# Two loads and a batch's scores moved by some steps in a fused attention and gated feed-forward kernel

## The chip, the cores and the metric

One core of a Trainium2 chip runs the whole program. The metric is device time in microseconds of one execution; lower is better. The core has a matrix engine (TensorE, PE in the profile), VectorE (DVE), ScalarE (ACT), GpSimd (POOL) and SyncE (SP), which in this kernel issues all DMA transfers of the main loop, in program order, from one queue.

## The reference

Eight batches, 12 heads, 448 positions, head size 64, all float32. Scores of all heads are mixed by a 12 x 12 matrix before the softmax, the weights of all heads by another behind it; the result goes through a feed-forward part with a gate and two matrices behind it.

```python
scores = scale * np.matmul(q, k.transpose(0, 1, 3, 2))
scores = np.einsum('bhij,hg->bgij', scores, w_pre)
scores = scores - np.max(scores, axis=-1, keepdims=True)
attn = np.exp(scores)
attn = attn / (np.sum(attn, axis=-1, keepdims=True) + 1e-09)
attn = np.einsum('bhij,hg->bgij', attn, w_post)
x = np.matmul(attn, v)          # then heads side by side: 3584 x 768
a = x @ w1
b = x @ w2
out = (a * b @ w3) @ w_out
```

The feed-forward weights come from the host as 64-bit words, which the kernel itself turns into float32 and splits into two parts.

## The kernel before

**Steps.** The attention part runs in steps `n`, 45 for each batch (`NB`), in one loop at the end of `run`. A step stands for a tile of ten query rows of one batch, all 12 heads. Work goes through HBM once: the scores of two heads at a time are computed and stored to `raw_d`, and the tiles are read back with the heads on the partitions, so that one matmul mixes them.

**Score units.** `qk` (L165 to L187) computes one unit (b, p, c): batch b, head pair p, query block c of 128 rows (c = 3 takes the last 64 rows of two pairs). Eight matmul instructions (L173) fill two PSUM banks, two ScalarE copies (L178, L179) take them to an SBUF tile `st`, and a store to `raw_d` follows (L187; for c = 3 two stores, L184). The store is put on the list `later` and issued at the start of the next step. The second unit of a step uses banks 6 and 7, the first banks 0 and 1. The tile `st` has two buffers in the pool `kp`; units of the first batch with an odd p have two others, in `qp`. A batch has 21 units; six of the first one (c = 0) come before the loop.

**Their places.** `qks` lists the units of each step, `loads` the loads of their inputs (`kq`, L156), six steps ahead of the unit with c = 0. The first batch's other 15 units lie on steps 0 to 14. The second batch's begin at `first` and lie `per` steps apart: steps 11, 12, 13, 15, 16, 17, 19, 20, 21 and so on to 37. Later batches have 45 / 21 steps for a unit.

**Tiles.** Each even step begins with a fetch (L201) of two tiles from `raw_d`, four steps ahead of their use. `mix` (L219), `largest` (L226, VectorE), `exp` (L234, ScalarE), `scale` (L243 to L246), `post` (L259) and `put` (L273) then work on a pair of tiles over two to three steps.

**Values.** `load_v` (L285) loads the values of one head pair of the next batch on a list. Steps 6 to 11 each load one for the first batch; later ones are loaded when their predecessor was used for the last time. `av` (L300) uses them in steps 19 and 21 first.

**Weights.** Beside the attention, w3 and w_out are folded into one matrix (`psf`, L359) in the steps up to 48. Their words come in 40 loads (`cs`, L100), at most one a step, two steps ahead of the conversion, into three buffers. The conversion of one load is a ScalarE square (L106), four VectorE instructions (L116 to L120), a ScalarE cast and a GpSimd subtraction (L125, L126). A step with `av` takes none. From step 18 on the fold's matmuls are shared out by `shares`: each step gets a number that levels the TensorE work, with a weight of 3.7 for a score unit, 5.1 for an `av` and 9.3 for the odd steps' `post`; before, they follow the conversions (`there`). Step 50 (`SWITCH`) ends the fold; from step 53 the experts (`eg`) take its place.

**Order in one step**, as far as it matters here: fetch (even steps); everything on `later` (stores of the step before); the other inputs of the first batch or `load_v`; `load_kq`; the load of weight words; conversion; fold matmuls and `exp`; `av`; `post` and `mix` (odd steps); the step's score units. The kernel gives the order of all engines by hand: nothing is reordered behind it.

Of the kernel before, what the change touches and what calls it, by code (L numbers as in the profile page):

```python
# [17 lines left out]
HP = H // 2  # L18
IB = 10
GI = H * IB  # L20
NB = -(-S // IB)
# [28 lines left out]
class Kernel:  # L50
# [689 lines left out]
    def run(self):  # L740
# [64 lines left out]
        for n, u in enumerate([(0, p, c) for c in (1, 2) for p in range(HP)] + [(0, p, 3) for p in range(1, HP, 2)]):  # L805
            qks[n] = [u]
        for b in range(1, B):
            first, per = (11, 28 / 21) if b == 1 else ((b - 1) * NB - 6, NB / 21)
            units = [(b, p, c) for g in range(0, HP, 2) for p, c in [*itertools.product((g, g + 1), range(3)), (g + 1, 3)]]
            for i, (b, p, c) in enumerate(units):  # L810
                n = int(first + i * per) | (b > 1)
                qks.setdefault(n, []).append((b, p, c))
                if c == 0:
                    loads.setdefault(max(n - 6, 0), []).append((b, p))
        for b in range(B):
            for a in range(NG):
                for g in range(HP):
                    n = (b * NB + (a + 1) * GB + 3) | 1
# [25 lines left out]
        for pair in range(ONE // 2, B // 2 - 1):  # L844
            first = P_AT if pair == ONE // 2 else 2 * NB * (pair + 1) + 13
# [5 lines left out]
        def advance(count):  # L851
            nonlocal done
            for _ in range(min(count, total - done)):
                next(background)
                done += 1
                self.age += len(self.ends) > 0
                if self.age > 2:
                    self.do_ends()

        def there(p):  # L860

            f, r = divmod(p - 3 - 2 * KF, 3)
            return 2 * KF * 3 * (1 + f) + (0, 9, 18)[r] if f >= 0 else min(max(3 * (p - 3), 0), KF * 3)
# [3 lines left out]
        def others(p):  # L867
            nc.sync.dma_start(self.kqs[0, p][:, QT + S:], self.kq0[p][:, QT + S:])
# [19 lines left out]
        for n in range(N + 6):  # L888
            self.step, third = n, False
            if n == GB + 1:  # L890
                self.close("qp")
                self.xp = [self.pool("xp0", 1)]
            if n == SWITCH:
                assert done == total
                next(background, None)
                self.do_ends()
                self.do_soon()
                self.do_later()
                assert not fold_pieces
                self.close("fp")  # L900
                self.wp = self.pool("wp", 5, side="right")
                self.up = self.pool("up", 1, side="right")
                self.xp.append(self.pool("xp1", 1, side="right"))
                background, total, done = self.experts(phases), (E_1 + E_2) * ONE + P_1 * (B - ONE) // 2, 0
            if n == LATE:
                assert done >= E_1
                self.close("xp0", "cx")
                self.xq, self.cb = self.pool("xq", 2), self.pool("cb", 1)
            if n == PAIR:

                assert done >= 2 * E_1 + E_2 and unit_pieces is None and not self.jobs and not self.ys
                self.do_ends()
                self.do_soon()
                self.do_later()
                self.pairs, self.w_ahead = True, 4
                self.close("xp1", "cb", "xq", "cs")
                self.xq = self.pool("xq", 2)
                self.up2 = self.pool("up2", 1, side="right")
                self.free += range(N_UP, NS)
                setup = self.pair_setup(phases)  # L920
            if PAIR <= n < PAIR + 7:
                next(setup, None)
            m, odd = divmod(n, 2)
            if not odd and LF <= n + LF < N:
                self.fetch(m + LF // 2)
            self.do_later()
            if n + 3 < HP:
                others(n + 3)
            elif HP <= n < 2 * HP:
                self.load_v()  # L930
            for x in loads.get(n, []):
                self.load_kq(*x)

            p, pieces = self.n_made - 1 if fold_pieces else 2 * KF + 3 * KF, None
            if avs.get(n):
                pass
            elif fold_pieces:
                f = (self.n_made - 1 - 2 * KF) // 3
                if f < 2 or done >= 2 * KF * 3 * (f - 1):
                    pieces = fold_pieces  # L940
                    if next(pieces, self) is self:
                        fold_pieces = pieces = None
            if m < SETS:
                if odd:
                    self.scale(m)
                else:
                    self.largest(m)
            self.do_soon()
            if pieces:
                next(pieces)  # L950
            elif unit_pieces and not fold_pieces and not avs.get(n):
                ahead = 1 if n < SWITCH else 2 * done // (3 * K1) + 4 + (done > 0)
                if n_pieces < ahead:
                    n_pieces += 1
                    if next(unit_pieces, self) is self:
                        unit_pieces = None
                    else:
                        next(unit_pieces)
                        third = True
            now = share.get(n, 0)  # L960
            if n < SWITCH:

                wanted += now
                now = max(min(there(p), KF * 3 + wanted) - done, 0)
            self.do_sums()

            advance(now // 2)
            self.do_ends()
            if not odd and m < SETS:
                self.exp(m)  # L970
            advance(now - now // 2)
            for x in avs.get(n, []):
                self.av(*x)
            self.do_ends()
            if odd and 1 <= m <= SETS:
                self.post(m - 1)
            if odd and m + 1 < SETS:
                self.mix(m + 1)
            self.do_ends()
            for i, x in enumerate(qks.get(n, [])):  # L980
                self.later.append(self.qk(*x, (6, 7) if i else (0, 1)))
            if third:
                next(unit_pieces)
# [67 lines left out]
```

## Time and profile before

| | |
|---|---|
| runs | 1459.4, 1459.1, 1453.31 us |
| median | 1459.1 us |
| the profiled execution | 1456.61 us, its span 1454.8 us |
| TensorE busy, 0 to 146 us | 113.73 us |
| TensorE busy, 146 to 437 us | 279.99 of 291 us |
| TensorE busy, 437 to 1200 us | 746.80 of 763 us |
| TensorE busy, 1200 to 1455 us | 249.61 of 255 us |
| mean granted clock of TensorE | 0.985 of full speed |

A profile is of one execution. The page gives the busy time of each engine and, in 40 slices, where in the span it lies; windows give the same for chosen stretches with the granted clock and what DMA moved. Waits are put down to what came last. "DMA share" is the mean busy share of the 16 DMA engines, and can be somewhat above 1. Matmul records are in part missing from a trace.

### The profile page before, as it was taken

The page shows a single profiled execution, that of the slowest core. Times are in us where ns is not written, and L with a number is a line of the kernel's source. Part 1 is how long each engine was busy: PE and PEld are TensorE (multiplying, and loading weights), DVE is VectorE, ACT ScalarE, POOL GpSimd, SP SyncE. Part 2 cuts the span into 40 slices and gives each one's busy share as a digit, 9 for nine tenths or more (in the row PEclk, how much of TensorE's full clock was granted, in tenths as well). Part 3 has the DMA queues.
Part 4 walks back from the last instruction along what each step waited for, and adds up shares of the span by engine and source line. Part 5 has one row for each costly group of instructions (what it writes and reads, how often), then busy time and mean ns, then how long its engine had stood idle before and what let it go on. Part 6 is the DMA issues. An engine that isn't in the chain of part 4 may idle for free.

```text
span 1454.8 us, 45722 instructions
## 1 busy us (share of the span) xinstructions
PE 1390.1 (96%) x18684; PEld 1059.4 (73%) x18684; DVE 739.0 (51%) x1497; ACT 833.1 (57%) x1952; POOL 620.7 (43%) x754
## 2 busy tenths in 40 slices
PE   5789998999999989999999999999999999999998
PEld 2357785776677667776777777777776777899988
DVE  4867565767644544432344445334444447334563
ACT  3876665777756656665555656656655546422231
POOL 1333232444324434632244445444335446446683
PEclk7989998999999999999999999999999999999999
DMA  8998789999999999999989988799879766698875
GB/s 256 365 319 274 237 267 287 311 336 307 316 288 353 348 343 319 368 338 314 311 266 291 319 278 280 234 312 350 288 230 285 236 179 214 206 332 263 240 229 173
DMA packets 203760, 416.86 MB, mean 287 GB/s; under 512 B 20528, under 2 KB 120112, under 8 KB 203472
## 3 DMA queue, kind: packets, MB, share of 16 engines
q1 hardware_dynamic: 203552, 413.94, 87.2%
q8 instruction: 149, 2.44, 0.7%
q14 instruction: 59, 0.48, 0.1%
HBM read 279.77 MB, written 134.09 MB: 284 GB/s over the span
## 4 chain that ended last, share of the span: by engine, by line
PE 78%; DMA 13%; DVE 5%; ACT 3%; issue 1%; SPq 0%; POOL 0%; DVEq 0%; ACTq 0%; POOLq 0%
PE e L701 20%; PE psa L300 10%; PE pso L259 10%; PE psm L219 8%; PE psq L173 7%; PE psf L359 5%; PE eg L521 4%; PE e2o L701 4%; PE e1o L701 4%; PE e3o L701 4%; DMA s_d<-s 3%; PE eo L552 3%; DMA cs<-wo 3%; DMA r<-raw_d 2%; DMA wu<-w_d 2%; ACT e L234 1%
## 5 line engine op out<-in xcount | busy, mean ns | idle before, releaser
L246 POOL TENSOR_SCALAR w<-wpo,ri 128x60 f32<-128x60 f32 x360 | 180.7, 518 | 489.0 <-DVE ri L244 465.8
L226 DVE TENSOR_REDUCE mn<-psm 128x1 f32<-128x448 f32 x360 | 207.8, 619 | 317.0 <-PE psm L219 316.6
L701 PE MATMUL e<-eh,wu 128*128 128x448 f32 x1008 | 297.3, 372 | 6.3 <-DVE c L655 3.2
L273 ACT COPY mt<-pso 128x480 f32<-128x480 f32 x352 | 197.8, 621 | 177.3 <-PE pso L259 177.1
L234 ACT ACTIVATE e<-psm,mn 128x448 f32<-128x448 f32 x360 | 226.6, 642 | 9.6 <-DVE mn L226 9.6
L219 PE MATMUL psm<-r,wsc 60*64 60x448 f32 (+1 forms) x1440 | 197.9, 557 | 32.1 <-ACT e L234 19.9
L701 PEld LDWEIGHTS e<-eh,wu 128*128 128x128 f32 x1008 | 188.0, 188 | 52.5 <-issue 27.4
L259 PEld LDWEIGHTS pso<-w,e 60*64 60x64 f32 x10080 | 174.5, 134 | 50.0 <-issue 44.0
L259 PE MATMUL pso<-w,e 60*64 60x60 f32 x10080 | 198.6, 224 | 0.1
L701 PE MATMUL e<-el,wu 128*128 128x448 f32 x504 | 187.1, 371 | 0.0
L173 PE MATMUL psq<-kq 64*64 64x448 f32 x1176 | 159.5, 546 | 0.6 <-ACT st L178 0.6
L300 PE MATMUL psa<-mt,v 128*64 128x150 f32 (+1 forms) x2304 | 156.9, 293 | 1.9 <-ACT st L178 1.9
L300 PEld LDWEIGHTS psa<-mt,v 128*64 128x64 f32 x2304 | 143.6, 137 | 17.9 <-issue 6.3
L655 DVE TENSOR_TENSOR c<-c,e 128x448 f32<-128x448 f32 x168 | 101.8, 618 | 87.6 <-PE e L701 82.8
L178 ACT COPY st<-psq 128x448 f32<-128x448 f32 x162 | 86.4, 533 | 68.8 <-ACT mt L273 32.8
L521 PE MATMUL eg<-xh,wu 128*128 128x448 f32 x384 | 118.8, 380 | 4.8 <-DMA wu<-w_d 4.8
L640 POOL TENSOR_TENSOR el<-x,eh 128x448 fp32r<-128x448 f32 x90 | 104.2, 1176 | 34.8 <-ACT eh L639 34.8
L701 PEld LDWEIGHTS e<-el,wu 128*128 128x128 f32 x504 | 94.9, 188 | 22.4 <-issue 14.1
L243 DVE TENSOR_SCALAR sa<-sm 128x2 f32<-128x2 f32 x180 | 35.9, 200 | 129.6 <-ACT e L234 129.0
L173 PEld LDWEIGHTS psq<-kq 64*64 64x64 f32 x1176 | 62.2, 136 | 53.8 <-issue 29.8
L521 PEld LDWEIGHTS eg<-xh,wu 128*128 128x128 f32 x384 | 71.8, 190 | 38.1 <-issue 25.3
L179 ACT COPY st<-psq 128x448 f32<-128x448 f32 x162 | 87.7, 541 | 0.0
(99 smaller groups left out, 2011.5 us busy)
## 6 DMA issues: line engine op xcount, KB each, us to landing
r<-raw_d SPq DMA_DIRECT2D x344, 210.0 KB, 4.9
raw_d<-st SPq DMA_DIRECT2D x138, 448.0 KB, 5.4
wu<-w_d SPq DMA_DIRECT2D x104, 384.0 KB, 6.4
wu<-s_d SPq DMA_DIRECT2D x96, 384.0 KB, 4.8
wu<-w_d SPq DMA_DIRECT2D x51, 512.0 KB, 5.6
kq<-kq SPq DMA_DIRECT2D x42, 448.0 KB, 6.2
wu<-s_d SPq DMA_DIRECT2D x36, 512.0 KB, 4.9
x<-x_d SPq DMA_DIRECT2D x72, 224.0 KB, 6.3
```

The source lines that it names most:

```text
L173: nc.tensor.matmul(ps[s][z * PP:(z + 1) * PP], t[rows, q:q + PP], t[rows, k:k + S], start=True, stop=True)
L219: nc.tensor.matmul(ps[s][c * PP:(c + 1) * PP, :S], self.wsc[k], r[k, c], start=True, stop=True)
L226: self.nc.vector.tensor_reduce(mn[:, s:s + 1], self.psm[m][s][:, :S], axis=AX.X, op=ALU.min)
L234: nc.scalar.activation(e, p[:, :S], AF.Exp, bias=mn[:, s:s + 1], scale=-1.0, accum_out=sm[:, s:s + 1])
L246: nc.gpsimd.tensor_scalar_mul(w2[:, s], self.wpo, ri[:, s:s + 1])
L259: nc.tensor.matmul(self.pso[c][z * PP:(z + 1) * PP, at:at + HK], e[k, j * PP:(j + 1) * PP], w2s[k, s], start=True, stop=True)
L273: self.nc.scalar.copy(dst.rearrange("p j g (s i) -> p j s g i", s=2), src)
L300: nc.tensor.matmul(self.psa[rows, g % 3, :W], v[:, j, rows], mt[:, j, 2 * g + s, :W], start=(j == 0), stop=(j == NJ - 1))
L521: nc.tensor.matmul(p, u[:, k % (K1 // 2), x], xs[y][:, k], start=(k == 0 and t == 0), stop=(k == K1 - 1 and t == 2))
L640: nc.gpsimd.tensor_tensor(lo, x, hi.bitcast(F32), op=ALU.subtract)
L655: nc.vector.tensor_tensor(a[out], a[to[0]], p, op=ALU.add)
L701: nc.tensor.matmul(p, w[:, k, x], ops[m, k][y], start=(k == 0 and t == 0), stop=(k == nk - 1 and t == 2))
```

## The change

The second batch's units begin at step 14 in place of 11 and lie 1.2 steps apart in place of 28 / 21 = 1.33. Their loads of `kq` move along. `load_v` is called in steps 11 to 16 in place of 6 to 11.

```diff
@@ -805,7 +805,7 @@
         for n, u in enumerate([(0, p, c) for c in (1, 2) for p in range(HP)] + [(0, p, 3) for p in range(1, HP, 2)]):
             qks[n] = [u]
         for b in range(1, B):
-            first, per = (11, 28 / 21) if b == 1 else ((b - 1) * NB - 6, NB / 21)
+            first, per = (14, 1.2) if b == 1 else ((b - 1) * NB - 6, NB / 21)
             units = [(b, p, c) for g in range(0, HP, 2) for p, c in [*itertools.product((g, g + 1), range(3)), (g + 1, 3)]]
             for i, (b, p, c) in enumerate(units):
                 n = int(first + i * per) | (b > 1)
@@ -926,7 +926,7 @@
             self.do_later()
             if n + 3 < HP:
                 others(n + 3)
-            elif HP <= n < 2 * HP:
+            elif HP <= n - 5 < 2 * HP:
                 self.load_v()
             for x in loads.get(n, []):
                 self.load_kq(*x)
```

## The prediction

> **What bounds the kernel now.** I read the page first, for the stage; then the DMA queue's timeline, for the places of the steps in time; then windows of two steps each; then the waits and the chain inside them.
>
> ```profile
> span 1454.8 us, 45722 instructions
> PE 1390.1 (96%) x18684; PEld 1059.4 (73%) x18684; DVE 739.0 (51%) x1497; ACT 833.1 (57%) x1952; POOL 620.7 (43%) x754
> PEclk7989998999999999999999999999999999999999
> DMA  8998789999999999999989988799879766698875
> ```
>
> TensorE is busy 96% of the span, so only its idle time and slow clock can be won: 64.7 us in all, and the change reaches only the beginning. Slices of 36.4 us: the steps that it touches, 5 to 38, lie in slices 2 to 6.
>
> ```profile
> 40.09 1.28 SPq L201 DMA_DIRECT2D r<-raw_d  x2
> ...
> 66.22 0.38 SPq L367 DMA_DIRECT2D w_d<-fz  x1
> ...
> 71.29 1.40 SPq L201 DMA_DIRECT2D r<-raw_d  x2
> 72.99 1.32 SPq L187 DMA_DIRECT2D raw_d<-st  x2
> ...
> 94.81 1.24 SPq L201 DMA_DIRECT2D r<-raw_d  x2
> ```
>
> Each even step begins with a fetch (L201). The two stores at 72.99 are those of step 11, the first step with two score units, and stores go out one step later; so 71.29 is step 12, 40.09 is step 4 and 94.81 step 18. Windows from fetch to fetch, with columns PE, PEld, DVE, ACT, POOL busy (instructions), granted clock, DMA share, GB/s:
>
> ```profile
> 40.09:47.81 7.72, 6.03 (x90) 2.82 (x87) 7.25 (x14) 6.50 (x16) 2.43 (x4) 1.00 1.01 363
> 47.81:55.60 7.79, 5.86 (x91) 2.82 (x87) 7.18 (x15) 6.89 (x17) 4.18 (x6) 1.00 1.02 351
> 55.60:61.85 6.25, 5.05 (x85) 2.46 (x85) 5.94 (x12) 5.45 (x14) 2.64 (x5) 1.00 1.04 363
> 61.85:71.29 9.44, 5.70 (x89) 2.86 (x90) 7.32 (x15) 7.53 (x18) 3.92 (x5) 1.00 1.04 377
> 71.29:79.46 8.17, 6.22 (x96) 2.90 (x94) 4.49 (x11) 6.22 (x16) 2.83 (x4) 1.00 1.03 378
> 79.46:87.83 8.37, 6.63 (x80) 4.18 (x80) 7.16 (x15) 7.56 (x19) 3.16 (x4) 0.59 1.02 376
> 87.83:94.81 6.98, 4.61 (x80) 2.31 (x80) 5.22 (x12) 5.02 (x13) 2.33 (x4) 0.96 1.02 351
> ```
>
> Two limits lie close together. DMA is saturated in all seven rows (share over 1, 351 to 378 GB/s). VectorE is nearly full in the first three (20.4 of 21.8 us) and has gaps from step 12 on. VectorE's beat shows which of the two rules:
>
> ```profile
> 42.98 1.15 DVE L226 TENSOR_REDUCE mn<-psm 128x1 f32<-128x448 f32 x2
> ...
> 63.31 1.14 DVE L226 TENSOR_REDUCE mn<-psm 128x1 f32<-128x448 f32 x2
> ...
> 96.51 1.14 DVE L226 TENSOR_REDUCE mn<-psm 128x1 f32<-128x448 f32 x2
> ```
>
> There is one such pair every two steps. From 42.98 to 63.31 three periods take 20.33 us, 3.39 us a step, VectorE's own pace. From 63.31 to 96.51 four periods take 33.20 us, 6.1 us more than that pace allows. What the extra time waits for (40 to 95 us; us in total, times, longest):
>
> ```profile
> DVE ca L116 <- DMA cs<-wo: 6.5, 6, 2.0
> DVE ca L116 <- DMA cs<-w3t: 1.5, 1, 1.5
> ...
> ACT st L178 <- DMA raw_d<-st: 0.4, 1, 0.4
> ```
> ```profile
> 65.57 8.33 DMA cs<-wo
> ...
> 74.96 7.50 DMA cs<-wo
> ...
> 84.77 6.40 DMA cs<-w3t
> ```
>
> The chain of this stage is a weight load that takes 6.4 to 8.3 us behind other transfers. So steps 4 to 10 go at VectorE's pace and build up a queue of transfers; steps 11 to 17 pay for it. From step 18 on TensorE is the bound:
>
> ```profile
> sum 110.45, PE 109.18 PEld 85.65 DVE 71.45 ACT 73.91 POOL 32.80; mean PE 15.60 PEld 12.24 DVE 10.21 ACT 10.56 POOL 4.69
> ```
>
> This is 105.04 to 215.49 us, steps 20 to 48: 1.3 us idle.
>
> **The change part by part.** The bytes of each transfer (view of DMA issues, 25 to 110 us; KB each, median time to landing):
>
> ```profile
> raw_d<-st SPq DMA_DIRECT2D x18, 448.0 KB, 5.6
> cs<-wo SPq DMA_DIRECT2D x14, 384.0 KB, 6.6
> r<-raw_d SPq DMA_DIRECT2D x22, 210.0 KB, 6.4
> kq<-kq SPq DMA_DIRECT2D x4, 448.0 KB
> ...
> v<-v SPq DMA_DIRECT2D x6, 256.0 KB, 6.3
> ...
> w_d<-fz SPq DMA_DIRECT2D x1, 384.0 KB
> ```
>
> In MB: a store of a score unit 0.459 (a c=3 unit goes in two halves of the same sum), a weight load 0.393, a fetch two times 0.215, a kq load 0.459, a v load 0.262.
>
> *Before, steps 4 to 17:* 14 weight loads 5.51, 7 fetches 3.01, 17 stores 7.80 (units of steps 3 to 16, two each in 11, 12, 13), kq loads at 5, 9, 14 1.38, v loads at 6 to 11 1.57, one fold store 0.39. Sum 19.66 MB in the 54.72 us from 40.09 to 94.81: 359 GB/s, which agrees with the windows.
>
> *After:* the second batch's units fall on 14 to 18, 20 to 24, 26 to 30, 32 to 36 and 38. Stores issued in steps 4 to 17: 15 in place of 17. The kq loads move to 8, 11, 16, 20, 24, 28: still three by step 17, the fourth after it. The six v loads move to 11 to 16. Sum 18.74 MB, 0.92 less.
>
> What is that worth? By bytes alone 0.92 MB / 359 GB/s = 2.6 us. But the v loads go from the half that VectorE bounds into the half that DMA bounds. Split at step 10, after the change: steps 4 to 10 hold 8.14 MB, 22.7 us of transfers, under 7 x 3.39 = 23.7 us of VectorE, so VectorE rules and 1 us of DMA goes unused; steps 11 to 17 hold 10.60 MB, 29.5 us, over 23.7, so DMA rules. Together 53.2 us against 54.7: 1.5 us. I take **2 us won**, between 1.5 and 2.6. The bounds of this term: VectorE's pace through all 14 steps is 47.4 us, a gain of 7.3. On the other side, steps 4 to 10 no quicker than now (40.09 to 66.2, the first SP row of step 11, so 26.1 us) and 10.60 MB at the slowest row, 351 GB/s, 30.2 us: 56.3, a loss of 1.6.
>
> *What is paid back.* Steps 18 and later get 17 units in place of 15. TensorE has no slack there, and each unit's eight matmuls are in the chain with
>
> ```profile
> 115.16 0.75 PE psq L173 x8
> ```
>
> so 2 x 0.75 = **1.5 us lost**. In steps 11 and 13 the second unit lay in TensorE idle time. If the later stage had idle time to take them, it would be 1.3 us of its 110 at most, so the bounds are 0.2 and 1.5.
>
> *What costs nothing.* The fold's matmuls are spread by the planner over steps 18 to 48 by weights of the units (step 18 gets 16 in place of 19); their number is the same, and TensorE is full either way. By the guard on `done` one conversion drops from step 25, and the last weight conversions and first expert weight loads come a step later, 46 to 48 in place of 45 to 47; experts begin at step 53, which is the cover: if it went, a late load costs up to the 8.33 us of the chain's row. The v loads end at step 16; tiles 0 to 2 are first read at step 19, 3 to 5 at step 21: two and more steps of cover at 3.39 us or more, against 6.3 us to landing. The first kq load is six steps ahead of its unit, as now. The last unit with c=0 comes at step 34 (now 33), and the fetch that reads it at step 40.
>
> *The sum:* -2.0 + 1.5 = **-0.5 us**, with ends of -7.3 + 0.2 = -7.1 and 1.6 + 1.5 = +3.1.
>
> **The clock** is the one term that the sum has not. Windows of 2 us, TensorE alone (busy, clock, DMA share, GB/s), and two groups of the fold:
>
> ```profile
> 82.00:84.00 2.00, 2.00 (x45) 0.50 1.02 382
> ...
> 94.00:96.00 2.00, 2.00 (x13) 0.56 1.00 358
> ```
> ```profile
> 95.40 4.59 PE L359 MATMUL psf<-fo,fw 128*128 128x384 f32 x19
> ```
> ```profile
> 216.11 3.57 PE L359 MATMUL psf<-fo,fw 128*128 128x384 f32 x19
> ```
>
> The clock fell to half twice in this stage, after TensorE gaps while it waited for copies. The second dip lay on the path: the same 19 matmuls took 4.59 us in place of 3.57, 1.0 us. The Trainium skill, "TensorE: Matmul & The Clock Gate", section "What's actually happening", says that the clock halves after an idle activity window and comes back only after a busy one. The rows above agree in kind, and the rule speaks against this change: it takes work from TensorE in steps 11 to 13, which are already short of it. That is a rival below.
>
> **The rivals.**
>
> *Full release.* The queue never builds, VectorE's pace holds to step 17 and the second dip is gone: -7.1 - 1.0 = -8.1 at best, -4 in the middle. For it: the seven VectorE waits (6.5 + 1.5 us) are all on these loads. Against it: 10.60 MB in seven steps can't move in 23.7 us at any rate that the rows show (378 GB/s: 28.0 us). Time 1453.9; chance 0.20, of which 0.07 for over 0.5%.
>
> *Slower: two "st" buffers.* From step 14 every second-batch unit copies into a tile with two buffers, and a copy waits for the store of two units back. On ScalarE the max-exponent pass and the other copies queue behind it, and TensorE waits for those. Now 7 of 21 units stand two steps behind the one whose buffer they need; after, 12 do. The price of one wait is bounded by nothing and
>
> ```profile
> ACT st L178 <- DMA raw_d<-st: 1.4, 1, 1.4
> ```
>
> (94.81 to 218 us; the unit of step 17). Three such waits in steps 16 to 18 give 4.2, less the 1.8 already paid: +2.4. If all 12 wait, 16.8 - 1.8 - 0.5 = +14.5, 1472.4. It decides where a store's landing and the copy pair (5.6 + 1.0 us) outlast two steps. Against it: this is the only such wait after step 17, though units at 21, 25, 29, 33 and 37 stand two steps apart now. Chance 0.05 for the full price, 0.05 for the three.
>
> *Half clock.* If steps 10 to 17 run at half clock, the 4.61 us of TensorE work of the lightest pair becomes 9.2, over the 8.24 us that a pair takes now ((94.81 - 61.85) / 4): 4 x 1.0 = +3.8, and 1.5 for the later stage: +5.3, 1463.2. By the page's rule this is where it would go if the gaps fill whole windows; in steps 4 to 9 TensorE had gaps too (5.05 of 6.25 us busy) and kept a clock of 1.00. Chance 0.08, of which 0.01 over 0.5%.
>
> *The change does not do what it says:* if a buffer held the moved loads where they are now, -0.5 would become 0, which no measurement tells from the forecast; it has no chance of its own.
>
> **How the numbers follow.** The profiled execution took 1456.61 us (its span is 1454.8, 1.8 us lie around it); the three other runs 1453.31, 1459.1 and 1459.4, median 1459.1, 2.5 above it. The median of all four is 1457.9, to which I apply the sum: **1457.4 us**. Chances: the forecast (-3 to +3) 0.62, full release 0.20, two buffers 0.10, half clock 0.08. The range: 1457.9 - 7.1 = 1450.8 at the low end, and 1463.2 at the high end; left out are the best of the full release and the full price of the buffers, about 0.12, and scatter. A measurement of this kernel tells about 0.5%, 7.3 us, from no change: faster by more 0.07, slower by more 0.06 (0.05 buffers, 0.01 clock), within it 0.87.
>
> **What would show it.** Right: steps 4 to 10 at 3.39 us with a DMA share under 1; the VectorE waits for weight loads still there, but from step 13 or 14 on; the fetch of step 18 about 2 us earlier, that of step 50 within 1 us of where it is now. Wrong: the waits for weight loads gone altogether (full release); new waits of ScalarE's L178 for stores after step 18 (buffers); a granted clock near 0.5 in steps 10 to 17. If the fetch of step 18 moves by 2 us and the time by over 5, the cause lies behind step 50, where I see nothing changed.

## The result and the profile after

The changed kernel takes 1462.38 us (median of 11 runs, 1456.45 to 1467.61), the kernel before 1454.91 us in the same series (11 runs, 1452.58 to 1459.43). The ratio, estimated from all of these runs, is 1.0044, 95% interval 1.0026 to 1.0063: slower by 0.44% of 1454.9, 6.4 us (3.8 to 9.2); the two medians lie 7.5 us apart. Forecast were 0.5 us less, and 1457.4 us in all, from 1450.8 to 1463.2. The measured time lies between these ends, but that is luck: the upper end stood for half clock all through steps 10 to 17, and there the clock was 0.95 (60.52 to 92.80 us).

The page of the profiled execution after (1463.27 us):

```profile
span 1461.5 us, 45714 instructions
PE 1394.0 (95%) x18684; PEld 1058.2 (72%) x18684; DVE 740.4 (51%) x1497; ACT 834.8 (57%) x1952; POOL 618.8 (42%) x754
PEclk8999999999999999999999999999999999999999
DMA  8988789999989999999988998799979766698775
```

TensorE is busy 3.9 us longer for the same 18684 matmuls, and idle 2.8 us longer. Since every even step begins with a fetch, the rows of SyncE's queue show where that comes in. A fetch marks SyncE's place in the program; TensorE can be ahead of it (in the changed kernel the fold of step 18 begins at 91.74 us, before the fetch at 92.80). The fetches of steps 18, 20 and 40, in two executions of each kernel (r1 and r2 are the second ones), in us from the span's start:

| fetch of step | before | before, r1 | after | after, r2 | mean after less mean before |
|---|---|---|---|---|---|
| 18 | 94.81 | 97.89 | 92.80 | 95.39 | -2.3 |
| 20 | 105.04 | 107.86 | 105.93 | 109.21 | +1.1 |
| 40 | 186.71 | 189.68 | 191.37 | 194.61 | +4.8 |
| 18 to 20 | 10.23 | 9.97 | 13.13 | 13.82 | +3.4 |
| 20 to 40 | 81.67 | 81.82 | 85.44 | 85.40 | +3.7 |

Behind step 50 the executions of one kernel drift apart by 2 us and more (the fetch of step 350: 1233.65 and 1231.45 us for before, 1240.34 and 1242.40 for after). From step 50 to step 350 the 16 traces of this case take 998 to 1014 us, and both the shortest (e9) and the longest (e10) have the moved units. So the traces place 4.8 us of the 6.4; the rest lies inside the interval.

**Steps 18 and 19.** TensorE in the changed kernel, from its timeline (start, duration, instructions; in brackets the idle time before and who ended it):

```profile
91.74 3.05 PE L359 MATMUL psf<-fo,fw 128*128 128x384 f32 x16
95.12 1.41 PE L173 MATMUL psq<-kq 64*64 64x448 f32 x8 [0.33 <-ACT st L178]
99.14 4.96 PE L300 MATMUL psa<-mt,v 128*64 128x150 f32 x48 [2.61 <-ACT st L178]
```

The same place before:

```profile
95.40 4.59 PE L359 MATMUL psf<-fo,fw 128*128 128x384 f32 x19
99.92 3.28 PE L300 MATMUL psa<-mt,v 128*64 128x150 f32 x48
```

Before, step 18 had no score unit and the values (`av`, psa) followed the fold without a gap. Now the unit of step 18 lies between. Its two banks are 0 and 1, `av` accumulates in bank 0, and so it waits for the copy of that unit. The wait is 2.61 us, and behind it the 48 matmuls take 4.96 us in place of 3.28: the granted clock had fallen. Why the copy came so late, from ScalarE's timeline after:

```profile
89.82 0.53 ACT L178 COPY st<-psq 128x448 f32<-128x448 f32 x1 [0.43 <-DMA raw_d<-st]
...
94.53 0.53 ACT L178 COPY st<-psq 128x448 f32<-128x448 f32 x1 [0.77 <-DMA raw_d<-st]
94.96 0.54 ACT L179 COPY st<-psq 128x448 f32<-128x448 f32 x1
95.39 0.53 ACT L125 CAST fw<-cx 128x384 fp32r<-128x384 f32 x1
97.00 0.43 ACT L106 ACTIVATE cm<-cs 128x256 f32<-128x256 f32 x1 [1.08 <-DMA cs<-w3t]
97.33 0.62 ACT L234 ACTIVATE e<-psm,mn 128x448 f32<-128x448 f32 x1
...
98.55 0.53 ACT L178 COPY st<-psq 128x448 f32<-128x448 f32 x1
```

These are steps 16, 17 and 18. The copies of the units of 16 and 17 wait for a store to free one of two buffers; that of 18 then stands, in program order, behind a square that waits for weight words and behind two exponent passes. ScalarE at the same place before:

```profile
97.18 0.53 ACT L178 COPY st<-psq 128x448 f32<-128x448 f32 x1 [1.43 <-DMA raw_d<-st]
97.61 0.54 ACT L179 COPY st<-psq 128x448 f32<-128x448 f32 x1
...
98.45 0.45 ACT L106 ACTIVATE cm<-cs 128x256 f32<-128x256 f32 x1
```

Here too the copy of the unit of 17 waits for a store, and longer. But the square of step 18 finds its words there, no copy of a unit stands behind it, and the copies end at 98.15, under the fold's 19 matmuls, behind which `av` begins at 99.92.

**Steps 20 to 39.** Windows from fetch to fetch, of after and then of before (PE, PEld, DVE, ACT, POOL busy; clock, DMA share, GB/s):

```profile
92.80:105.93 13.13, 10.20 (x133) 7.85 (x132) 4.32 (x12) 6.18 (x15) 1.83 (x3) 0.87 0.76 268
105.93:191.37 85.44, 83.21 (x1139) 61.70 (x1139) 53.28 (x110) 56.06 (x133) 23.03 (x34) 1.00 0.78 247
```
```profile
105.04:186.71 81.67, 80.40 (x1127) 62.11 (x1123) 53.71 (x109) 54.47 (x131) 23.81 (x34) 1.00 0.80 254
```

TensorE's busy time grows by 2.8 us and its idle time by 1.0 (2.23 against 1.27). The idle time is waits of psa for a copy, three in place of two (the unit of step 34 now stands ahead of the `av` of step 35):

```profile
170.27 3.28 PE L300 MATMUL psa<-mt,v 128*64 128x150 f32 x48 [0.96 <-ACT st L178]
```

### The profile page after: what moved, and what is told of

Its sections match the earlier page's. It is cut to its first block, busy times and chain, and to the rows that moved or that the text cites. A ratio compares the mean times of both kernels' runs of the same rounds, so it can differ in the third digit from the quotient of the medians.

```text
span 1461.5 us, 45714 instructions
## 1 busy us (share of the span) xinstructions
PE 1394.0 (95%) x18684; PEld 1058.2 (72%) x18684; DVE 740.4 (51%) x1497; ACT 834.8 (57%) x1952; POOL 618.8 (42%) x754
## 4 chain that ended last, share of the span: by engine, by line
PE 80%; DMA 11%; DVE 3%; ACT 2%; issue 1%; SPq 1%; POOL 1%; DVEq 0%; ACTq 0%; POOLq 0%
PE e L701 20%; PE psa L300 10%; PE pso L259 10%; PE psm L219 9%; PE psq L173 7%; PE eg L521 6%; PE psf L359 4%; PE eo L552 4%; PE e2o L701 4%; PE e1o L701 4%; PE e3o L701 4%; DMA cs<-w 2%; DMA r<-raw_d 2%; DMA wu<-w_d 2%; DMA s_d<-s 1%; ACT e L234 1%
## 5 line engine op out<-in xcount | busy, mean ns | idle before, releaser
L178 ACT COPY st<-psq 128x448 f32<-128x448 f32 x162 | 86.6, 535 | 73.2 <-PE psq L173 33.8
```

## The experiments

All times are ratios to the kernel before, measured beside it on the same chip. e6, e7, e8, e10, r1 and r2 were executed once each, so only places in their traces are compared.

**The two halves of the change, each alone.** e1 moves only the values, e2 only the scores.

```diff
 e1: -            elif HP <= n < 2 * HP:
     +            elif HP <= n - 5 < 2 * HP:
 e2: -            first, per = (11, 28 / 21) if b == 1 else ...
     +            first, per = (14, 1.2) if b == 1 else ...
```

> The kernel before with the values loaded in steps 11 to 16, the scores unmoved. Theory A (the loss comes from score units that now stand in front of an av step, at 18 above all, and in even steps): no loss here; the fetch of step 18 within 1.5 us of that of before, from step 18 to step 20 10.2 us as before, TensorE without a wait ahead of the first psa group; time within 2 us of before. Theory B (the values, loaded late, crowd out the weight loads of steps 16 to 18, and these are what the engines wait for at step 18): from step 18 to step 20 about 13 us, time 3 us or more over before.

> The kernel before with the second batch's scores from step 14 on, 1.2 steps apart, the values loaded in steps 6 to 11. Theory A: nearly the whole loss is here: a wait of over 1.5 us ahead of the first psa group, from step 40's fetch 4 to 6 us later than in before, time 3 to 7 us over before. Theory B: step 18 to 20 in 10 to 11 us, and only the 1.5 us of the two units in the later stage, less what is won before step 18: within 1 us of before.

e1: 0.9997 (0.9977 to 1.0018); step 18 to 20 in 8.62 us, shorter than the 10.2 expected (the fold's 19 matmuls took 3.57 us there, without the half clock of before); no wait ahead of the first psa group. e2: 1.0034 (1.0015 to 1.0052); step 18 to 20 in 13.60 us, the fetch of step 40 at 192.17, and in its timeline

```profile
100.27 4.95 PE L300 MATMUL psa<-mt,v 128*64 128x150 f32 x48 [2.78 <-ACT st L178]
```

The loss belongs to the scores; the late values play no part in it (theory B falls). e1's fetch of step 18 came at 97.04, 2.2 us after that of before, outside the 1.5 us expected; but the second execution of before had it at 97.89, so this says nothing.

**The unit of step 18 moved behind `av`, and all units clear of the steps ahead of `av`.** To the changed kernel:

```diff
 e3: -                n = int(first + i * per) | (b > 1)
     +                n = int(first + i * per) | (b > 1) | (b == 1 and i == 4)
 e4: -                n = int(first + i * per) | (b > 1)
     +                n = int(first + i * per) | 1 if b > 1 else (14, 15, 16, 17, 19, *range(21, 32), 33, 35, 36, 37, 38)[i]
```

> The changed kernel with one unit moved from step 18 to step 19, behind the av of that step. Theory A: the wait ahead of the first psa group and the half clock in it go, 2.6 + 1.7 us less some tenths; the fetch of step 20 comes 1.5 to 2.5 us earlier than in before (in the changed kernel 0.9 later), and time is 3 to 4.5 us under the changed kernel. Theory B: the wait stays, since the weight load is as late: 12.5 us or more from step 18 to step 20.

> The changed kernel with the second batch's units on steps 14 to 17, 19, 21 to 31, 33 and 35 to 38: none in a step ahead of an av step (18, 20, 32, 34), seven in even steps from 18 on in place of eleven. Theory A: no wait of a psa group for L178 in the first 220 us, the fetch of step 40 1 to 3 us earlier than in before (4.7 later in the changed kernel); time 5 to 8 us under the changed kernel, 0 to 3 under before. If the loss were only the two more units on a full TensorE, the fetch of step 40 stays 1 us or more after that of before.

e3: 1.0011 (0.9987 to 1.0035), step 18 to 20 in 7.83 us, the wait 0.48 us and the 48 matmuls at 3.28:

```profile
96.36 3.28 PE L300 MATMUL psa<-mt,v 128*64 128x150 f32 x48 [0.48 <-ACT st L178]
```

The fetch of step 20 comes 3.6 us earlier than in before, more than expected. e4: 0.9982 (0.9963 to 1.0002), step 18 to 20 in 8.37 us, no wait of psa for L178, the fetch of step 40 at 185.73, 1.0 us earlier than in before, the least that was expected. Moving one unit by one step takes back most of the loss (e2, in the same series, had 1.0034).

**Is a unit ahead of `av` enough?** e5 is the kernel before with one unit of step 17 moved to 18.

```diff
                 n = int(first + i * per) | (b > 1)
+                n += b == 1 and i == 5
```

> The kernel before with one unit of step 17 moved to step 18, nothing else. Theory A (a unit in front of an av step holds bank 0, and its copy stands on ScalarE behind the square of late weight words): a wait of 2 to 3 us ahead of the first psa group, at half clock behind it; the fetch of step 20 3 to 5 us later than in before, time 2 to 5 us over. Rival (the wait needs the units of steps 14 to 17 in a row, or the later kq loads): the wait is under 1 us and the fetch of step 20 less than 1.5 us later.

No: 0.9999 (0.9968 to 1.0029), the fetch of step 20 0.7 us earlier than in before. There is a wait, but a shorter one, and the clock holds:

```profile
99.19 3.28 PE L300 MATMUL psa<-mt,v 128*64 128x150 f32 x48 [1.48 <-ACT st L178]
```

The wait is 1.48 us, between the two theories' numbers (2 to 3 and under 1), and costs nothing in sum, presumably because step 17 lost its unit. So theory A was incomplete. The rival, units in a row, remained; in a row they wait for buffers. In e5 the square of step 18 does not wait for words either, as in before.

**What makes the copy late.** e7 takes no weight words in step 18; e9 has three score buffers in place of two; e10 has both. To the changed kernel:

```diff
 e7:  -            if avs.get(n):
      +            if avs.get(n) or n == 18:
 e9:  -            st = (...).tile([128, 2, S], F32, tag="st", ..., bufs=2)
      +            st = (...).tile([128, 2, S], F32, tag="st", ..., bufs=2 if b == 0 and p % 2 else 3)
```

> The changed kernel, but step 18 takes no weight words: no load, no square and no conversion in that step, all later ones a step later. The unit of step 18 stays ahead of av. If its copy is late because it stands on ScalarE behind a square that waits for words: the wait ahead of the first psa group falls from 2.6 us to under 0.8, no half clock in it (3.3 us for 48 in place of 5.0), the fetch of step 20 3 to 5 us earlier than in the changed kernel. If sharing bank 0 alone makes the wait: it stays over 2 us.

> The changed kernel with three buffers in place of two for the score tiles of the pool kp. Theory C (the copies of units 16 to 18 wait for the stores of two units back, 0.4 to 1.6 us each, and so the first av group waits for the copy of unit 18): no wait of L178 for a store in the first 105 us; the wait ahead of psa falls from 2.6 us to 1.0 to 2.0, with late weight words still in front of the copy; the fetch of step 20 1 to 2.5 us earlier than in the changed kernel, time 1 to 3 us under it. If the buffers play no part: the wait stays at 2.2 us or more.

> The changed kernel with three such buffers and no weight words taken in step 18. Theory C with late words as the second cause: both are gone, the wait ahead of the first psa group under 0.8 us, its 48 matmuls in 3.3 us, step 18 to 20 in under 10 us (13.1 in the changed kernel, 12.5 without the words alone). If sharing bank 0 alone makes the wait, it stays over 2 us.

| | wait ahead of psa | its 48 matmuls | step 18 to 20 |
|---|---|---|---|
| after, r2 | 2.61, 2.60 | 4.96, 5.84 | 13.13, 13.82 |
| e7, no words | 2.17 | 4.95 | 12.51 |
| e9, three buffers | 4.22 | 5.67 | 13.58 |
| e10, both | 1.18 | 3.28 | 8.78 |

Neither alone helps: both misses. The traces show why. In e7, without the square, the copies of units 17 and 18 wait for stores:

```profile
96.86 0.53 ACT L178 COPY st<-psq 128x448 f32<-128x448 f32 x1 [1.64 <-DMA raw_d<-st]
...
100.45 0.53 ACT L178 COPY st<-psq 128x448 f32<-128x448 f32 x1 [1.37 <-DMA raw_d<-st]
```

In e9, with a third buffer, the copy of unit 17 is on time and the square of step 18 waits longer:

```profile
94.06 0.54 ACT L178 COPY st<-psq 128x448 f32<-128x448 f32 x1
...
98.15 0.43 ACT L106 ACTIVATE cm<-cs 128x256 f32<-128x256 f32 x1 [2.72 <-DMA cs<-w3t]
...
99.71 0.52 ACT L178 COPY st<-psq 128x448 f32<-128x448 f32 x1
```

They are two waits in series for the same crowded transfers, and what one gives up the other takes. With both away the step pair is back under its old length, in the one execution of e10:

```profile
96.49 3.28 PE L300 MATMUL psa<-mt,v 128*64 128x150 f32 x48 [1.18 <-ACT st L178]
```

The wait left, 1.18 us, is over the 0.8 expected; as in e5, a unit directly ahead of `av` keeps one. The `av` groups of steps 21, 33 and 35 wait 0.64 us in the same trace, and the copy ahead of them waits only for its matmuls; so about half of the 1.18 us seems to come from bank 0 and half from ScalarE's order. e9's time is 1.0038 (1.0014 to 1.0063), no better than the change itself, and one wait for a store, 0.64 us at 78.44, was left in spite of the third buffer. e10's 1464.48 us is no evidence on this stage: its trace is level with before at step 40 (186.72 against 186.71) and loses 7 us behind step 70 (1241.44 against 1233.65 at step 350). Of its edits only the third buffer is at work there, and e9, which has it too, reached step 350 at 1231.28.

**What a unit costs on a full TensorE.** e6 moves four units of before from odd to even steps; e8 moves its units of steps 16 and 17 to the free steps 22 and 26.

```diff
 e6: +                n += b == 1 and n in (21, 25, 29, 37)
 e8: +                n = {16: 22, 17: 26}.get(n, n) if b == 1 else n
```

> The kernel before with the units of steps 21, 25, 29 and 37 moved to the even steps 22, 26, 30 and 38 behind them. If a unit in an even step, between two runs of the fold, costs 0.4 us more than one behind the mix of an odd step, the fetch of step 40 comes 1.2 to 2 us later against that of step 20 than in before (81.7 us there); if a unit costs the same 1.15 us anywhere, within 0.5 us.

> The kernel before with the units of steps 16 and 17 moved to the free steps 22 and 26, neither ahead of an av step. It prices the term of two more units on a full TensorE: by the chain's row 2 x 0.75 = 1.5 us from the fetch of step 20 to that of step 40 (81.7 us in before); by the pairs of steps with one and with two units 2 x 1.15 = 2.3 us. Before step 18 0.92 MB less goes through: its fetch 1 to 2.6 us earlier.

The windows from the fetch of step 20 to that of 40, of e6 and of e8:

```profile
108.05:191.53 83.48, 82.17 (x1130) 61.24 (x1122) 52.91 (x109) 55.00 (x131) 21.90 (x34) 1.00 0.77 242
```
```profile
107.60:191.20 83.60, 82.33 (x1141) 62.12 (x1137) 53.72 (x108) 56.52 (x135) 23.01 (x34) 1.00 0.82 260
```

Against 81.67 before, e6 adds 1.8 us with no unit more: 0.45 us for each move from an odd to an even step. e8 adds 1.9 us for two units, 0.97 each. But this window has lost two of the fold's matmuls (217 in place of 219), which the planner put behind step 40. From the fetch of step 20 to that of step 48 the fold has 322 in both kernels, and e8 takes 112.73 us in place of 110.45: 2.3 us, 1.14 for each unit. That is the higher of the two prices. In e6 the same stretch gives 0.43 for a move. e8's fetch of step 18 did not come earlier but at 97.97; its program is that of before up to step 16, whose fetch was already 3.0 us late (90.81 against 87.83), so this execution says nothing of the first term.

**The scatter.**

> The kernel before once more, for the spread of one execution against another by places. If the first 18 steps are the same from run to run, its fetch of step 18 lies within 0.5 us of 94.81; the kernels with the same first steps so far lay at 94.6 and 97.8, so I expect 94 to 98, and from step 20 to 40 81.7 us within 0.3.

> The changed kernel once more. If the loss at step 18 belongs to the program: step 18 to 20 12.5 to 13.6 us, step 20 to 40 85.4 us within 0.5, the wait ahead of the first psa group 2 to 3 us. What its times behind step 50 differ from the first execution is scatter.

The numbers stand in the table at the top. Steps 0 to 18 spread by 3 us from run to run; steps 20 to 40 repeat within 0.15 us; the loss from step 18 to 20 belongs to the program, though r2's 13.82 us are 0.2 over what was expected. r1's fetch of step 18 came 3.1 us after that of the first execution: the first 18 steps do not repeat.

**Is there a net gain once the units stand clear?** e12 repeats e4; e11 is e4 with three score buffers.

> The kernel of e4 once more. If the gain before step 18 is net once the units stand clear of the av steps: 1 to 3 us under before again, and the fetch of step 40 0 to 3 us under the median 188.2 of the two executions of before. If e4 was scatter: the ratio lies over 1.000.

> The kernel of e4 with three score tiles in the pool kp. If the copies' waits for stores in steps 16 and 17 cost the stage something: 0.5 to 2 us under e4 at the fetch of step 20, and no wait of L178 for a store in the first 105 us. If transfers bound the stage in any case: the same within 1 us.

e12: 0.9956 (0.9932 to 0.9981); e11: 0.9971 (0.9947 to 0.9995). The fetch of step 40 in e4, e12 and e11: 185.73, 184.42 and 184.89 us, 2.5 to 3.8 us under the mean of before (188.2). The intervals of e12 and e11 lie under 1, that of e4 ends at 1.0002: this version is faster than the kernel before, by 0.2 to 0.4% (6.4 us less in e12's series, more than the 1 to 3 expected, and 2.6 in e4's). The third buffer adds nothing that can be told: the fetch of step 20 is 0.9 us earlier than in e4 and 0.4 later than in e12, and one wait for a store, 1.2 us, was left in spite of it, against what was expected. e12 from step 18 to 20 and from 20 to 40:

```profile
94.26:101.52 7.26, 7.15 (x128) 6.17 (x130) 5.40 (x13) 5.09 (x13) 1.86 (x3) 1.00 1.04 354
101.52:184.42 82.90, 82.90 (x1145) 62.04 (x1137) 52.78 (x109) 56.62 (x135) 22.99 (x34) 1.00 0.82 265
```

Step 20 to 40 has no idle time at all, and steps 18 and 19 run at full clock. The later stage is still 1.2 us longer than in before: 2.5 us more TensorE work and 1.3 less idle time.

## Why the prediction was wrong

*What bounds the kernel.* Transfers and VectorE up to step 17: right as far as it goes. "From step 18 on TensorE is the bound" was wrong for steps 18 and 19. The row quoted for it began at step 20. In before, step 18 was full because the fold's 19 matmuls covered ScalarE's delay (a wait of 1.43 us for a store) and because it had no unit whose copy came later still.

*The first term, 2.0 us won before step 18.* It fits within scatter. Its signs came: from step 4 to step 10 a step took 3.37 us, with a DMA share of 0.99 (40.30 to 60.52), and of the 6.0 us that VectorE waited for weight loads 4.8 came from about step 13 on (75.61 us). All kernels with the units on 14 to 17, the values late and two buffers have the fetch of step 18 at 92.80, 95.39 (after, r2), 93.65 (e3), 94.44 (e4), 94.26 (e12) and 95.31 (e7), mean 94.3; those with the first 18 steps of before at 94.81, 97.89 (r1) and 97.78 (e6), mean 96.8: 2.5 us. With e5, which differs from before in step 17 alone (94.55), the second mean is 96.3 and the gain 1.9. It is not seen in pairs of single runs, and three or four executions on one side don't prove it.

*"What is paid back", 1.5 us: this is the step that failed,* in two ways.

First, it counted the new unit of step 18 as 0.75 us of TensorE work and nothing else. It stands ahead of `av`, shares bank 0 with it, and its copy came last of all in ScalarE's row of waits: 3.4 us from step 18 to 20. The "What costs nothing" paragraph listed step 18's 16 fold matmuls in place of 19 and did not ask what those 19 had hidden. The waits of 0.63 us ahead of psa at steps 21 and 33, where a unit already stood ahead of `av`, were in the trace of before.

Second, the size. In the later stage the two units, the shift of three units from odd to even steps and one more wait ahead of `av` cost 3.7 us: 2.8 of TensorE time and 1.0 idle. The price of a unit was 1.14 us (e8), not 0.75: two cost 2.3 us in place of 1.5. The 0.75 us of the chain's row is a unit that follows `mix` in an odd step. In an even step it cuts a run of fold matmuls in two, which is my reading of the higher price, not shown by itself. Between the two fetches TensorE has 136 score matmuls in place of 124, one and a half units more and not two (in before that of step 19 still ran behind the fetch of step 20, and half of that of step 39 behind the fetch of step 40). Three and a half have gone from odd to even steps: 1.5 x 1.14 + 3.5 x 0.45 = 3.3 us, 0.5 over the 2.8. So these prices are rough. The windows of before had the price of a unit: steps 24 and 25, with 15 + 7 fold matmuls and two units, took 7.68 us, steps 22 and 23, with 19 + 7 and one unit, 7.27. With 0.19 us for each of the four matmuls less (3.57 us for 19) that is 1.17 for the unit.

*The rivals.* "Two st buffers" was the rival on the right side, and half of the mechanism: the copies of units 16 and 17 did wait for stores (0.43 and 0.77 us; 1.64 in e7). But it put the point of decision at the length of two steps and the price at one wait each. The price came from what stood behind: `av` in bank 0, and the half clock. "TensorE waits for those" was said there and not followed to the instruction that waits. "Half clock" was looked for in steps 10 to 17, where it came for 3.4 us (79.28 to 82.69; in before for 6.8 us, 80.57 to 87.40); the one that cost time came in step 19. The wait ahead of the second dip of before was for exponent passes (1.80 us), where "The clock" says copies. "Full release" did not come.

*What would show it.* The line "the fetch of step 50 within 1 us of where it is now" showed the failure: 231.77 against 226.88. The sign that was named for the buffers, new waits of L178 for stores after step 18, did not appear (one of 0.77 at step 17); the sign to ask for was who waits for L178.

Open: the split of the 1.2 us left in e10 between bank 0 and ScalarE's order is only an estimate; a kernel with `av` in a bank of its own wasn't tried. Nor is the remainder behind step 50 (1.6 us of the 6.4) settled.

## What to carry to other kernels

Before work is moved into a gap of a planner's list, look at what comes next in the same PSUM bank: a small matmul group ahead of a large one makes the large one wait for the small one's copy, and that copy for everything ahead of it on its engine. Work that fills a step also hides the delays of other engines; when its amount changes, ask what it covered. And when two waits in series come from one crowded resource, taking away either can show nothing: test both together before a cause is dropped.

## What the runs showed of the hardware

The clock fell after short waits. TensorE alone in the changed kernel, in windows of 1 us (busy, clock, DMA share, GB/s):

```profile
96.00:97.00 1.00, 0.53 (x7) 1.00 1.03 384
97.00:98.00 1.00, 0.00 (x0) 1.00 1.08 309
98.00:99.00 1.00, 0.00 (x0) 1.00 1.05 311
99.00:100.00 1.00, 0.86 (x12) 0.88 1.04 319
100.00:101.00 1.00, 1.00 (x12) 0.50 0.93 351
...
103.00:104.00 1.00, 1.00 (x16) 0.91 0.07 29
```

The idle time was 2.6 us. The clock went to half only when work had begun again, at about 99.8, and was back at about 103.2, 3.4 us later. With the waits of 2.17 us (e7) and 4.22 us (e9, while the wait still ran) it fell as well; with 1.48 us (e5) and 1.18 us (e10) it held. But no length decides: e5 had another wait of 2.25 us, at 90 to 92 us, and kept 1.00 through it.

In each of the 16 traces the changes of the clock lie whole multiples of 3.41 us apart, and the TensorE work in the stretch of 3.41 us ahead of such a place tells the cases apart: 0.80 us ahead of the fall in the changed kernel (96.35 to 99.76), 1.57 in r2, 1.24 in e7 and 1.09 in e9, against 1.83 or more in every stretch from 84 to 101 us of e5 and e10. No single figure parts all traces: 1.49 us held in e9 (from 74.49), and 2.28 us were followed by a fall in e4 (from 88.32).

The Trainium skill, "TensorE: Matmul & The Clock Gate", section "What's actually happening", gives a window of about 3.4 us, of idle time for the fall and of work for the return, and says that the window runs freely. The spacing of 3.41 us, and the return after one such stretch of full work, agree. The fall does not need an idle window here: the stretches ahead of it held 0.80 to 1.57 us of work, so waits well under 3.4 us can bring half clock.

The other surprise: the stage that transfers bound spreads by 3 us between executions of one program, and the stage that TensorE bounds repeats within 0.15 us.
